# Linear-attention and SwiGLU block on one core: statistics of the first norm shared out anew, shift columns and modulations placed elsewhere

## The chip, the cores and the metric

The kernel runs on one NeuronCore of a Trainium2 chip. The metric is the device time in microseconds (us), the median of several runs. TensorE multiplies matrices and transposes, VectorE and ScalarE do element-wise work and sums, GpSimd some small operations, and SyncE (SP) issues nearly all DMAs, in order, on one queue. Each engine carries out its own instructions in the order in which they were written and waits on semaphores for the others.

## The reference

One sequence of 2048 tokens with 1024 features in bf16 passes through one block with adaptive layer norms:

```python
mod = (_silu(c) @ w_mod).reshape(c.shape[0], 6, 1, -1)
sa, ca, ga, sb, cb, gb = ...                      # shift, scale, gate, twice
h = _layernorm(x) * (1 + ca) + sa
x = x + ga * _A_ref(h, A_wqkv, A_wo)              # linear attention, 32 heads of 32
h = _layernorm(x) * (1 + cb) + sb
x = x + gb * _B_ref(h, B_w_gate, B_w_up, B_w_down)  # SwiGLU, 3584 wide
```

In the attention `phi(t) = where(t > 0, t + 1, exp(t)) + 1e-6` is applied to q and k, `kv` is the sum over the tokens of `phi(k)` times `v`, and the output is `phi(q) @ kv` over `phi(q)` times the sum of `phi(k)`, then times `wo`.

## The kernel before, in words

The 2048 tokens lie in 16 tiles of 128 (`XRES[:, st, :]`), four tiles make a chunk of 512 tokens. The program is a straight list of instructions: a small recorder (`_Prog`, line 176 for nearly all instructions, which is why the profile gives one line for them) finds the dependences from the tiles read and written and puts in the semaphores. A PSUM bank counts as one object: when another engine touched it last, the next one waits for that. The order on each engine is the order in which the Python code calls `P.pe`, `P.act`, `P.dve`, `P.pool` and `P.dma`; nothing reorders it.

**Head.** The four tiles of chunk 0 are loaded first, then in turns the scale columns' weights (`wca`, two halves), the q weights (`wq`), and the shift columns' weights (`wsa`, upper half first). TensorE runs warm-up matmuls on a zero tile. VectorE takes the statistics of tiles 0, 2 and 3 with `bn_stats`, ScalarE those of tile 1 with two passes over it (`act_stats`: one sums x, one sums x squared). GpSimd takes the power -1/2 of the variance. Tiles 0 and 1 are normed on ScalarE, 2 and 3 on VectorE. TensorE transposes each normed tile into PSUM (`tile_transposes`, 8 transposes a tile, banks 4 to 7), between these come the matmuls that make the first scale columns (`mod_sc`: one column for each 128 features, 8 matmuls of one column each), and VectorE copies the transposed features out with the scale (`h0_first`) or raw (`raw_copy`).

**q of chunk 0** (`q_phase_chunk0`). Seven of eight groups of 128 q features collect in seven banks at once, feature tile (`dt`) by feature tile, because the weights and the columns come in late. Bank 0 holds the columns. The q matmuls use h with the scale alone for `dt` 0 to 5; what the shift adds is a bias, made by one-column matmuls (`bias_mm`) and added when q is evacuated (`phi_evac`: exponential and relu on ScalarE, two operations on VectorE for each pair of groups). For `dt` 6 and 7 the shift is put in at once (`h0_scale`). After the eighth group VectorE adds the shifts to the other six tiles (`h0_shift`), since the k groups of chunk 0 need the whole h. In this stretch ScalarE takes the sums of tile 4 and VectorE those of tiles 5, 6 and 7; VectorE norms them, and a DMA transpose on SP (`th_dma`) puts each into `HT[:, 1]`, the h of chunk 1. Entries in `qside` and `kside` are carried out after the q or k group of that number.

**k of chunk 0, then chunks 1 to 3.** Each group is eight matmuls of 512 columns. After the second k group `kside` has the eight modulations of chunk 1 (`th_mod(1, dt)`: scale and shift in one VectorE operation each). Banks are taken in the turn 1, 2, 3, 4, 6, 7, 5, 0.

**Output projection.** For each token tile `st` 16 matmuls, two evacuations on VectorE with the residual (`wo_res`), and beside them the columns of the second norm: the weighted sum of weight rows (`macc`), a DMA transpose, a reduction on VectorE (`mod_red`) at `st` 8. At `st` 7 the first chunk of the second norm is normed and transposed by DMA; at `st` 8 GpSimd modulates it (`th2_mod`). The SwiGLU part follows: per chunk 28 pairs of gate and up groups, then the down projection.

Of the kernel before, what the change touches and what calls it, by code (L numbers as in the profile page):

```python
# [262 lines left out]
def bass_adaLN_cond__linear_attn_block__swiglu_ffn__prompt_kernel(  # L263
# [20 lines left out]
    EPS = 1e-5  # L284

    with ExitStack() as es:
# [117 lines left out]
        def sa_load(p):  # L404
            P.dma("wsa%d" % p, WSA[:, :, 512 * p:512 * p + 512], wmv[:, :, 512 * p:512 * p + 512])
# [12 lines left out]
        sa_load(0)  # L418
# [74 lines left out]
        def th_mod(ch, dt):  # L493
            buf = ch % 2
            if dt % 2 == 0 or ch == 1:
                P.dve("tensor_scalar", out=HT[:, buf, dt, :], in0=HT[:, buf, dt, :], scalar1=MODCOL[:, 0, dt:dt + 1],
                      scalar2=MODCOL[:, 1, dt:dt + 1], op0=ALU.mult, op1=ALU.add)
            else:
                P.act("activation", out=HT[:, buf, dt, :], in_=HT[:, buf, dt, :], func=ACT.Identity,
                      scale=MODCOL[:, 0, dt:dt + 1], bias=MODCOL[:, 1, dt:dt + 1])  # L500
# [3 lines left out]
        def mod_sc(w, c0, ms):  # L504
            for m in ms:
                for kt in range(NDT):
                    P.pe("matmul", out=PS[:, 0, c0 + m:c0 + m + 1], lhsT=w[:, kt, m * 128:(m + 1) * 128],
                         rhs=SILUC[:, kt:kt + 1], start=mod_first[0], stop=(kt == NDT - 1), skip_group_check=True)
                    mod_first[0] = False
# [14 lines left out]
        def h0_shift(dt):  # L524
            P.dve("tensor_scalar", out=HT[:, 0, dt, :], in0=HT[:, 0, dt, :], scalar1=MODCOL[:, 1, dt:dt + 1],
                  scalar2=None, op0=ALU.add)
# [47 lines left out]
        def act_stats(st, c0=0, mid=None):  # L574
            n = (D - c0) // 512
            junk0 = HT[:, 1, 0:2, :] if st < 8 else JUNK1
            for fn_, sc_, acc_ in ((ACT.Identity, 1.0 / D, SUMX), (ACT.Square, D ** -0.5, SUMSQ)):
                P.act("activation", out=junk0[:, 0:n, :], in_=XRES[:, st, c0:D].rearrange("p (a b) -> p a b", a=n),
                      func=fn_, scale=sc_, accum_out=acc_[:, st:st + 1])
                if mid is not None:  # L580
                    mid()
                    mid = None
# [13 lines left out]
        s0_, s2_, s3_ = ln1_stats_ops(0), ln1_stats_ops(2), ln1_stats_ops(3)  # L596
# [6 lines left out]

        def act_xn(st, mean):
            P.dve("tensor_scalar", out=NMR[:, st:st + 1], in0=mean, scalar1=RSTD[:, st:st + 1],
                  scalar2=-1.0, op0=ALU.mult, op1=ALU.mult)
            P.act("activation", out=XRES[:, st, :], in_=XRES[:, st, :],
                  func=ACT.Identity, scale=RSTD[:, st:st + 1], bias=NMR[:, st:st + 1])
# [7 lines left out]

        warm(13, bank=3)
        act_stats(1)
        for f in s0_:
            f()  # L620
        ln1_rstd1(0)
        s2_[0]()
        s2_[1]()
        act_xn(0, MV[:, 0, 0:1])
        tile_transposes(0)
        warm(5, bank=3)
        act_var(1)
        P.pool("tensor_tensor", out=RSTD[:, 1:2], in0=VE[:, 1:2], in1=NEGHALF[:, 0:1], op=ALU.pow)
        P.pool("tensor_scalar", out=NMR[:, 1:2], in0=SUMX[:, 1:2], scalar1=RSTD[:, 1:2], scalar2=-1.0,
               op0=ALU.mult, op1=ALU.mult)  # L630
        P.act("activation", out=XRES[:, 1, :], in_=XRES[:, 1, :], func=ACT.Identity, scale=RSTD[:, 1:2],
              bias=NMR[:, 1:2])
        s2_[2]()
        ln1_rstd1(2)
        s3_[0]()
        s3_[1]()
        s3_[2]()
        ln1_rstd1(3)
        ln1_xn(2)
        mod_sc(WCA, 8, range(2))  # L640
        tile_transposes(1, 2)
        ln1_xn(3)
        fin_ca(0, 2)
        tile_transposes(3)
# [100 lines left out]
        def q_phase_chunk0(side):  # L745
# [7 lines left out]
            for nt in range(7):  # L753
                if nt == 3:
# [5 lines left out]
            act_stats(4)  # L760
            for nt in range(7):
                if nt == 4:
                    mod_sc(WSA, 0, range(6, 8))
                    fin_sa(6, 2)
                    for dt in (6, 7):
                        h0_scale(dt)
                q_part(nt, qb[nt], (4, 5))
            mod_sc(WSA, 0, range(4, 6))
# [5 lines left out]
            for nt in range(7):  # L774
                if nt == 1:
                    mod_sc(WSA, 0, range(4))
                    fin_sa(0, 4, True)
                    ln_ops[1][0]()
                    ln_ops[1][1]()
                if nt == 4:  # L780
# [3 lines left out]
            ln_ops[1][2]()  # L784
            ln1_rstd1(5)
            for f in act_mv_ops(4):
                f()
            neg_rstd(4)
# [4 lines left out]
            for dt in (4, 5):  # L793
                h0_shift(dt)
            ln1_xn(5)
            th_dma(5)
            for dt in range(4):
                h0_shift(dt)
            ln1_xn(4)
            th_dma(4)  # L800
# [12 lines left out]
        def ln_x1(jj):  # L813
            for f in ln_ops[jj]:
                f()
            ln1_rstd1(4 + jj)
        for f in ln_ops[2]:
            add(qside, 1, f)
        for f in ln_ops[3]:
            add(qside, 1, f)  # L820
        add(qside, 1, lambda: ln1_rstd2(6))
        for jj in range(2, 4):
            add(qside, 3, lambda jj=jj: ln1_xn(4 + jj))
            add(qside, 3, lambda jj=jj: th_dma(4 + jj))
        for dt in range(NDT):
            add(kside, 1, lambda dt=dt: th_mod(1, dt))
# [253 lines left out]
        for st in range(NST):  # L1080
# [16 lines left out]
            if st == 8:  # L1097
# [6 lines left out]
            if st == 8:  # L1104
# [110 lines left out]
```

## Time and profile before

| what | before |
|---|---|
| median of 3 runs (lowest, highest) | 828.66 us (828.06, 828.85) |
| span of the profiled execution | 827.0 us |
| busy: TensorE, VectorE, ScalarE, GpSimd | 817.0, 310.8, 197.3, 40.7 us |
| mean granted TensorE clock | 1.000 |
| first to last instruction, 0 to 10 us: TensorE busy | 7.27 us |
| 10 to 30 us | 19.34 us |
| DMA read and written | 100.67 MB, 4.33 MB |

The profiled execution's own time is its span; the timed runs lie some 1.65 us above it. A timeline line gives the start, the time that a merged group of equal instructions took together, the engine, the operation with the tiles that it writes and reads, its shape, how many, and in brackets how long the engine had been idle before it and what ended that. `PEld` is TensorE's weight load, which is issued ahead of its matmul.

### The profile page before, as it was taken

To read this page: it belongs to the slowest core of one execution; us is meant where nothing else is said; L and a number is where in the kernel's file an instruction comes from. 1 tells how busy PE (TensorE), PEld (TensorE's weight loads), DVE (VectorE), ACT (ScalarE), POOL (GpSimd) and SP (SyncE) were. 2 spreads that over 40 slices of the span, in tenths; PEclk is the share of its full clock that TensorE was granted. 3 is DMA by queue.
4 is the path that set the end of the run, shared out by engine and by line. 5 is a ranking of instruction groups with operands and counts; after the bars stand their busy time and mean duration, and the time that the engine had idled before them with its cause. 6 is when DMAs were issued, how large, how long until landed. Compare 5 with 4: busy or idle time off the path is not lost.

```text
span 827.0 us, 10428 instructions
## 1 busy us (share of the span) xinstructions
PE 817.0 (99%) x4244; PEld 376.1 (45%) x4323; DVE 310.8 (38%) x664; ACT 197.3 (24%) x336; POOL 40.7 (5%) x59
## 2 busy tenths in 40 slices
PE   8999999999999999999999999999999999999998
PEld 4544444444444444444444444444444444444444
DVE  5798988476945521111221112122111211221111
ACT  4658643123241111011111101111110111111011
POOL 1010000000130000030000003000000300000000
PEclk9999999999999999999999999999999999999999
DMA  9969665856697995700455570045557004553000
GB/s 317 283 151 225 156 169 144 185 166 200 164 256 234 289 256 153 175 27 23 133 149 152 154 177 29 20 128 153 152 153 185 26 19 124 153 153 87 0 26 26
DMA packets 199360, 119.32 MB, mean 144 GB/s; under 512 B 57992, under 2 KB 183056, under 8 KB 199312
## 3 DMA queue, kind: packets, MB, share of 16 engines
q1 hardware_dynamic: 199296, 118.65, 53.7%
q8 instruction: 34, 0.56, 0.3%
q14 instruction: 14, 0.11, 0.0%
q10 hardware_dynamic: 16, 0.00, 0.0%
HBM read 100.67 MB, written 4.33 MB: 127 GB/s over the span
## 4 chain that ended last, share of the span: by engine, by line
PE 95%; DMA 2%; DVE 1%; SPq 1%; issue 1%; ACT 0%; DVEq 0%; ACTq 0%
PE ps L176 95%; DMA wsa<-in_w_mod_dram 2%; DVE acc L176 1%; SPq L176 1%; DVE pkt L176 0%; DVE e L176 0%; DVE pqt L176 0%; ACT e L176 0%; DVE xres L176 0%; DVE ht L176 0%; DVEq L247 0%; ACTq L247 0%
## 5 line engine op out<-in xcount | busy, mean ns | idle before, releaser
L176 PE MATMUL ps<-h2t,gug 128*128 128x512 bf16 x878 | 210.1, 379 | 0.9
L176 PE MATMUL ps<-h2t,guu 128*128 128x512 bf16 x878 | 209.9, 379 | 0.9
L176 DVE TENSOR_TENSOR at<-sg,ps 128x512 bf16<-128x512 bf16 x112 | 77.0, 688 | 282.7 <-PE ps L176 270.5
L176 ACT ACTIVATE sg<-ps 128x512 bf16<-128x512 f32 x112 | 66.9, 597 | 309.7 <-PE ps L176 298.3
L176 PEld LDWEIGHTS ps<-h2t,guu 128*128 128x128 bf16 x896 | 87.7, 98 | 105.7
L176 PEld LDWEIGHTS ps<-h2t,gug 128*128 128x128 bf16 x896 | 87.6, 98 | 105.5
L176 PE MATMUL ps<-wd_a,at 128*128 128x512 bf16 (+1 forms) x502 | 111.9, 377 | 0.5
L176 PE MATMUL ps<-ht,wqk 128*128 128x512 bf16 x499 | 110.5, 379 | 1.0 <-issue 0.2
L176 PE MATMUL ps<-wd_b,at 128*128 128x512 bf16 (+1 forms) x377 | 84.7, 377 | 0.4
L176 PEld LDWEIGHTS ps<-wd_a,at 128*128 128x128 bf16 x512 | 50.1, 98 | 59.7
L176 DVE TENSOR_TENSOR ut<-att,gb_b 128x512 bf16<-128x512 bf16 (+1 forms) x32 | 13.9, 435 | 167.2 <-ACT att L176 167.2
L176 PEld LDWEIGHTS ps<-ht,wqk 128*128 128x128 bf16 x512 | 49.4, 98 | 59.0 <-DVE ht L176 0.7
L176 ACT ACTIVATE att<-ps 128x512 bf16<-128x512 f32 (+1 forms) x32 | 17.4, 591 | 182.1 <-PE ps L176 182.1
L176 PEld LDWEIGHTS ps<-wd_b,at 128*128 128x128 bf16 x384 | 37.5, 98 | 44.7
L176 PE MATMUL ps<-pk,xres 128*128 128x512 bf16 x250 | 55.4, 379 | 0.6 <-issue 0.5
L176 PE MATMUL ps<-mw,pqt 128*128 128x512 bf16 x249 | 55.5, 379 | 0.5 <-issue 0.2
L176 POOL TENSOR_SCALAR h2t<-h2t,modcol 128x512 bf16<-128x512 bf16 x32 | 26.3, 837 | 383.4 <-DMA h2t<-xn 383.4
L176 ACT ACTIVATE e<-ps 128x512 bf16<-128x512 f32 x56 | 33.2, 604 | 31.9 <-PE ps L176 20.2
L176 PEld LDWEIGHTS ps<-mw,pqt 128*128 128x128 bf16 x256 | 24.7, 98 | 30.2 <-issue 0.5
L176 PEld LDWEIGHTS ps<-pk,xres 128*128 128x128 bf16 x256 | 24.7, 98 | 29.9 <-issue 0.9
L176 ACT ACTIVATE junk<-xres 128x1024 bf16<-128x1024 bf16 x24 | 25.4, 1058 | 34.5 <-DVE xres L176 34.2
L176 DVE SCALAR_TENSOR_TENSOR xres<-ps,xres 128x512 bf16<-128x512 f32 x32 | 21.4, 688 | 11.8 <-PE ps L176 11.6
(107 smaller groups left out, 337.9 us busy)
## 6 DMA issues: line engine op xcount, KB each, us to landing
gug<-in_B_w_gate_dram SPq DMA_DIRECT2D x56, 512.0 KB, 4.0
guu<-in_B_w_up_dram SPq DMA_DIRECT2D x56, 512.0 KB, 5.3
xres<-in_A_x_dram SPq DMA_DIRECT2D x20, 256.0 KB, 4.4
rb<-recip_den SPq DMA_DIRECT2D x8, 512.0 KB, 11.5
stgx<-in_w_mod_dram SPq DMA_DIRECT2D x2, 2048.0 KB, 9.7
wd_a<-in_B_w_down_dram SPq DMA_DIRECT2D x4, 1024.0 KB, 7.4
out_dram<-xres SPq DMA_DIRECT2D x31, 128.0 KB, 1.7
xres<-in_A_x_dram SPq DMA_DIRECT2D x3, 1024.0 KB, 7.1
```

Of the source, the lines that this page charges most:

```text
L176: return getattr(e, method)(**kw)
```

## The change

ScalarE sums tiles 0 and 2 of the first chunk and VectorE tiles 1 and 3; tile 0 is normed on ScalarE, the others on VectorE (`ln1_xn_sum` takes the mean from ScalarE's sum). The 13 + 5 warm-up matmuls become 16 in one run. In the q phase the last four scale columns are made one group later, the last two shift columns near the end of `dt` 4 and 5, the first four in two halves of four weight tiles, with the load of their weights in two DMAs, and the bias product one group later. ScalarE's first pass over tile 4 stays in place and its second one goes behind the second q evacuation; its scratch tile is another one. VectorE's statistics of tile 5 move behind the bias copy. The shifts of `dt` 2 and 3 go to GpSimd, and the norms and transposes of tiles 5 and 4 into the q evacuations. The modulation of chunk 1 moves from behind the second to behind the fourth k group, with `dt` 3 and 7 on GpSimd. In the output projection the reduction and the modulation of the second norm move from `st` 8 to `st` 9. Some helpers that are no longer called go.

```diff
@@ -401,8 +401,8 @@
 def ca_load(p):
     P.dma("wca%d" % p, WCA[:, :, 512 * p:512 * p + 512], wmv[:, :, D + 512 * p:D + 512 * p + 512])
 
-def sa_load(p):
-    P.dma("wsa%d" % p, WSA[:, :, 512 * p:512 * p + 512], wmv[:, :, 512 * p:512 * p + 512])
+def sa_load(p, k0=0, k1=8):
+    P.dma("wsa%d_%d" % (p, k0), WSA[:, k0:k1, 512 * p:512 * p + 512], wmv[:, k0:k1, 512 * p:512 * p + 512])
 
 def wq_load(i, n=1):
     P.dma("wq%d" % i, WQK[:, i:i + n, 0:D], wqkvv[:, i:i + n, 0:D])
@@ -415,7 +415,8 @@
 sa_load(1)
 wq_load(6)
 wq_load(7)
-sa_load(0)
+sa_load(0, 0, 4)
+sa_load(0, 4, 8)
 for j in range(2):
     P.dma("x1_%d" % j, XRES[:, 4 + j, :], xv[:, 4 + j, :])
 for i in (1, 0):
@@ -492,7 +493,10 @@
 
 def th_mod(ch, dt):
     buf = ch % 2
-    if dt % 2 == 0 or ch == 1:
+    if ch == 1 and dt in (3, 7):
+        P.pool("tensor_scalar", out=HT[:, buf, dt, :], in0=HT[:, buf, dt, :], scalar1=MODCOL[:, 0, dt:dt + 1],
+               scalar2=MODCOL[:, 1, dt:dt + 1], op0=ALU.mult, op1=ALU.add)
+    elif dt % 2 == 0 or ch == 1:
         P.dve("tensor_scalar", out=HT[:, buf, dt, :], in0=HT[:, buf, dt, :], scalar1=MODCOL[:, 0, dt:dt + 1],
               scalar2=MODCOL[:, 1, dt:dt + 1], op0=ALU.mult, op1=ALU.add)
     else:
@@ -501,9 +505,9 @@
 
 mod_first = [True]
 
-def mod_sc(w, c0, ms):
+def mod_sc(w, c0, ms, kts=range(NDT)):
     for m in ms:
-        for kt in range(NDT):
+        for kt in kts:
             P.pe("matmul", out=PS[:, 0, c0 + m:c0 + m + 1], lhsT=w[:, kt, m * 128:(m + 1) * 128],
                  rhs=SILUC[:, kt:kt + 1], start=mod_first[0], stop=(kt == NDT - 1), skip_group_check=True)
             mod_first[0] = False
@@ -521,8 +525,8 @@
     P.dve("tensor_scalar", out=HT[:, 0, dt, :], in0=HT[:, 1, dt, :], scalar1=MODCOL[:, 0, dt:dt + 1],
           scalar2=None, op0=ALU.mult)
 
-def h0_shift(dt):
-    P.dve("tensor_scalar", out=HT[:, 0, dt, :], in0=HT[:, 0, dt, :], scalar1=MODCOL[:, 1, dt:dt + 1],
+def h0_shift(dt, eng="dve"):
+    getattr(P, eng)("tensor_scalar", out=HT[:, 0, dt, :], in0=HT[:, 0, dt, :], scalar1=MODCOL[:, 1, dt:dt + 1],
           scalar2=None, op0=ALU.add)
 
 def bias_mm(dts):
@@ -571,15 +575,12 @@
 
 JUNK1 = T("junk1", 204 * KB, [128, 2, 512], BF16)
 
-def act_stats(st, c0=0, mid=None):
-    n = (D - c0) // 512
-    junk0 = HT[:, 1, 0:2, :] if st < 8 else JUNK1
-    for fn_, sc_, acc_ in ((ACT.Identity, 1.0 / D, SUMX), (ACT.Square, D ** -0.5, SUMSQ)):
-        P.act("activation", out=junk0[:, 0:n, :], in_=XRES[:, st, c0:D].rearrange("p (a b) -> p a b", a=n),
+def act_stats(st, passes=(0, 1)):
+    junk0 = HT[:, 1, 0:2, :] if st < 4 else JUNK1[:]
+    for i in passes:
+        fn_, sc_, acc_ = ((ACT.Identity, 1.0 / D, SUMX), (ACT.Square, D ** -0.5, SUMSQ))[i]
+        P.act("activation", out=junk0, in_=XRES[:, st, :].rearrange("p (a b) -> p a b", a=2),
               func=fn_, scale=sc_, accum_out=acc_[:, st:st + 1])
-        if mid is not None:
-            mid()
-            mid = None
 
 def act_mv_ops(st):
     return [
@@ -593,19 +594,13 @@
           op1=ALU.add)
     P.pool("tensor_tensor", out=RSTD[:, st:st + 1], in0=VE[:, st:st + 1], in1=NEGHALF[:, 0:1], op=ALU.pow)
 
-s0_, s2_, s3_ = ln1_stats_ops(0), ln1_stats_ops(2), ln1_stats_ops(3)
+s1_, s3_ = ln1_stats_ops(1), ln1_stats_ops(3)
 
 def act_var(st):
     P.dve("scalar_tensor_tensor", out=MV[:, st, 1:2], in0=SUMX[:, st:st + 1], scalar=SUMX[:, st:st + 1],
           in1=SUMSQ[:, st:st + 1], op0=ALU.mult, op1=ALU.subtract)
     P.dve("tensor_scalar", out=VE[:, st:st + 1], in0=MV[:, st, 1:2], scalar1=-1.0, scalar2=EPS, op0=ALU.mult,
           op1=ALU.add)
-
-def act_xn(st, mean):
-    P.dve("tensor_scalar", out=NMR[:, st:st + 1], in0=mean, scalar1=RSTD[:, st:st + 1],
-          scalar2=-1.0, op0=ALU.mult, op1=ALU.mult)
-    P.act("activation", out=XRES[:, st, :], in_=XRES[:, st, :],
-          func=ACT.Identity, scale=RSTD[:, st:st + 1], bias=NMR[:, st:st + 1])
 
 def tile_transposes(*js):
     for dt in range(NDT):
@@ -614,34 +609,39 @@
             P.pe("transpose", out=PSB[:, 4 + dt // 2, c:c + 128], in_=XRES[:, j, dt * 128:(dt + 1) * 128],
                  identity=IDENT[:])
 
-warm(13, bank=3)
-act_stats(1)
-for f in s0_:
+def ln1_xn_sum(st):
+    P.dve("tensor_scalar", out=XRES[:, st, :], in0=XRES[:, st, :],
+          scalar1=SUMX[:, st:st + 1], scalar2=RSTD[:, st:st + 1], op0=ALU.subtract, op1=ALU.mult)
+
+def pool_pow(st):
+    P.pool("tensor_tensor", out=RSTD[:, st:st + 1], in0=VE[:, st:st + 1], in1=NEGHALF[:, 0:1], op=ALU.pow)
+
+warm(16, bank=3)
+act_stats(0)
+for f in s1_:
     f()
-ln1_rstd1(0)
-s2_[0]()
-s2_[1]()
-act_xn(0, MV[:, 0, 0:1])
+ln1_rstd1(1)
+act_var(0)
+pool_pow(0)
+P.pool("tensor_scalar", out=NMR[:, 0:1], in0=SUMX[:, 0:1], scalar1=RSTD[:, 0:1], scalar2=-1.0,
+       op0=ALU.mult, op1=ALU.mult)
+act_stats(2)
+for f in s3_:
+    f()
+ln1_rstd1(3)
+P.act("activation", out=XRES[:, 0, :], in_=XRES[:, 0, :], func=ACT.Identity, scale=RSTD[:, 0:1],
+      bias=NMR[:, 0:1])
+act_var(2)
+pool_pow(2)
+ln1_xn(1)
+tile_transposes(1)
 tile_transposes(0)
-warm(5, bank=3)
-act_var(1)
-P.pool("tensor_tensor", out=RSTD[:, 1:2], in0=VE[:, 1:2], in1=NEGHALF[:, 0:1], op=ALU.pow)
-P.pool("tensor_scalar", out=NMR[:, 1:2], in0=SUMX[:, 1:2], scalar1=RSTD[:, 1:2], scalar2=-1.0,
-       op0=ALU.mult, op1=ALU.mult)
-P.act("activation", out=XRES[:, 1, :], in_=XRES[:, 1, :], func=ACT.Identity, scale=RSTD[:, 1:2],
-      bias=NMR[:, 1:2])
-s2_[2]()
-ln1_rstd1(2)
-s3_[0]()
-s3_[1]()
-s3_[2]()
-ln1_rstd1(3)
-ln1_xn(2)
+ln1_xn(3)
 mod_sc(WCA, 8, range(2))
-tile_transposes(1, 2)
-ln1_xn(3)
+tile_transposes(3)
+ln1_xn_sum(2)
 fin_ca(0, 2)
-tile_transposes(3)
+tile_transposes(2)
 mod_sc(WCA, 8, range(2, 4))
 h0_first(0, "dve")
 h0_first(1, "dve")
@@ -751,20 +751,21 @@
         for nt in nts:
             q_part(nt, qb[nt], dts)
     for nt in range(7):
-        if nt == 3:
+        if nt == 4:
             mod_sc(WCA, 8, range(4, 8))
             fin_ca(4, 4)
             for dt in (4, 5):
                 h0_scale_only(dt)
         q_part(nt, qb[nt], (2, 3))
-    act_stats(4)
-    for nt in range(7):
-        if nt == 4:
-            mod_sc(WSA, 0, range(6, 8))
-            fin_sa(6, 2)
-            for dt in (6, 7):
-                h0_scale(dt)
+    act_stats(4, (0,))
+    for nt in range(6):
         q_part(nt, qb[nt], (4, 5))
+    q_part(6, qb[6], (4,))
+    mod_sc(WSA, 0, range(6, 8))
+    fin_sa(6, 2)
+    for dt in (6, 7):
+        h0_scale(dt)
+    q_part(6, qb[6], (5,))
     mod_sc(WSA, 0, range(4, 6))
     fin_sa(4, 2, True)
     for nt in range(7):
@@ -772,32 +773,27 @@
             bias_mm((4, 5))
         q_part(nt, qb[nt], (6,))
     for nt in range(7):
-        if nt == 1:
-            mod_sc(WSA, 0, range(4))
+        if nt == 2:
+            mod_sc(WSA, 0, range(4), range(4))
+        if nt == 4:
+            mod_sc(WSA, 0, range(4), range(4, 8))
             fin_sa(0, 4, True)
-            ln_ops[1][0]()
-            ln_ops[1][1]()
-        if nt == 4:
+        if nt == 5:
             bias_mm(range(4))
             bias_fin()
         q_part(nt, qb[nt], (7,))
-    ln_ops[1][2]()
-    ln1_rstd1(5)
-    for f in act_mv_ops(4):
-        f()
-    neg_rstd(4)
     q_phi = lambda nt: phi_evac(qb[nt] if nt < 7 else 0, PQT[:, nt, 0:512], bias=BIASQ[:, nt:nt + 1])
     for i, dt in enumerate((4, 5, 0, 1, 2, 3, 6, 7)):
         P.pe("matmul", out=PS[:, 0, :], lhsT=WQK[:, dt, 896:1024], rhs=HT[:, 0, dt, :], start=(i == 0),
              stop=(i == 7))
-    for dt in (4, 5):
+    for f in ln_ops[1]:
+        f()
+    P.dve("tensor_scalar", out=VE[:, 5:6], in0=MV[:, 5, 1:2], scalar1=EPS, scalar2=None, op0=ALU.add)
+    for dt in (4, 5, 0, 1):
         h0_shift(dt)
-    ln1_xn(5)
-    th_dma(5)
-    for dt in range(4):
-        h0_shift(dt)
-    ln1_xn(4)
-    th_dma(4)
+    for dt in (2, 3):
+        h0_shift(dt, "pool")
+    pool_pow(5)
     for nt in range(8):
         q_phi(nt)
         for f in side.get(nt, []):
@@ -810,20 +806,23 @@
 qside, kside = {}, {}
 ln_ops = [ln1_stats_ops(4 + jj) for jj in range(4)]
 
-def ln_x1(jj):
-    for f in ln_ops[jj]:
-        f()
-    ln1_rstd1(4 + jj)
 for f in ln_ops[2]:
-    add(qside, 1, f)
+    add(qside, 0, f)
+add(qside, 0, lambda: ln1_xn(5))
+add(qside, 0, lambda: th_dma(5))
+add(qside, 1, lambda: act_stats(4, (1,)))
+add(qside, 1, lambda: act_var(4))
+add(qside, 1, lambda: pool_pow(4))
 for f in ln_ops[3]:
     add(qside, 1, f)
 add(qside, 1, lambda: ln1_rstd2(6))
+add(qside, 1, lambda: ln1_xn_sum(4))
+add(qside, 1, lambda: th_dma(4))
 for jj in range(2, 4):
     add(qside, 3, lambda jj=jj: ln1_xn(4 + jj))
     add(qside, 3, lambda jj=jj: th_dma(4 + jj))
 for dt in range(NDT):
-    add(kside, 1, lambda dt=dt: th_mod(1, dt))
+    add(kside, 3, lambda dt=dt: th_mod(1, dt))
 for jj, k in ((0, 3), (1, 4)):
     add(kside, k, lambda jj=jj: act_stats(10 + jj))
 q_phase_chunk0(qside)
@@ -1094,14 +1093,14 @@
         macc(STGX[0], kt)
     if st == 6:
         macc_split()
-    if st == 8:
+    if st == 9:
         mod_red()
         mod_fin_col(3, False)
     if st == 7:
         for jj in range(4):
             ln2_xn(jj)
         th2_dma()
-    if st == 8:
+    if st == 9:
         th2_mod()
     if st == 7:
         for q in range(4):
```

## The prediction, made before the changed kernel ran

> **What bounds the kernel now.** I read the page first, part 1 and the chain that ended last: TensorE is busy for 99% of the span and holds 95% of that chain.
>
> ```profile
> span 827.0 us, 10428 instructions
> ...
> PE 817.0 (99%) x4244; PEld 376.1 (45%) x4323; DVE 310.8 (38%) x664; ACT 197.3 (24%) x336; POOL 40.7 (5%) x59
> ...
> PE 95%; DMA 2%; DVE 1%; SPq 1%; issue 1%; ACT 0%; DVEq 0%; ACTq 0%
> ```
>
> So an edit pays only if it shortens or lengthens a place where TensorE stands still. Since matmuls overlap, those places show best in the timeline of its weight loads: a load that waits, right-hand brackets, marks them. Head, q phase, first k group of chunk 1 and the output projection:
>
> ```profile
> 7.28 0.15 PEld L176 LDWEIGHTS ps<-e,ident 128*128 128x128 bf16 x1 [0.28 <-issue]
> 8.64 0.45 PEld L176 LDWEIGHTS ps<-ident,xres 128*128 128x128 bf16 x8 [1.21 <-ACT xres L176]
> 9.04 0.80 PEld L176 LDWEIGHTS ps<-e,ident 128*128 128x128 bf16 x5
> 9.96 0.67 PEld L176 LDWEIGHTS ps<-siluc,wca 128*128 128x128 bf16 x16
> 10.56 1.35 PEld L176 LDWEIGHTS ps<-ident,xres 128*128 128x128 bf16 x24
> ...
> 21.40 0.47 PEld L176 LDWEIGHTS ps<-siluc,wsa 128*128 128x128 bf16 x16 [0.67 <-DMA wsa<-in_w_mod_dram]
> ...
> 24.04 0.47 PEld L176 LDWEIGHTS ps<-modtmp,wqk 128*128 128x128 bf16 x16 [0.42 <-DVE modcol L176]
> ...
> 45.83 0.55 PEld L176 LDWEIGHTS ps<-ht,wqk 128*128 128x128 bf16 x4 [0.23 <-DVE ht L176]
> ...
> 227.04 0.55 PEld L176 LDWEIGHTS ps<-mw,pqt 128*128 128x128 bf16 x4 [0.39 <-DVE xres L176]
> ```
>
> A load is normally issued one matmul (0.216 us at full speed) ahead, so the true stalls are smaller than the brackets: 0.34 us for the first shift columns, 0.09 for their bias product, 0.10 in the first k group of chunk 1, 0.27 at 227. First q matmul: 12.50; eighth q group: 28.69. Between 12.5 and 134 us TensorE has no other stall worth naming. All that can be removed here is about 1.2 us (with 0.36 from the head, below), 0.15% of the span. New stalls have no such ceiling.
>
> **Head, first norm.** TensorE's order before, from 8.64: 8 transposes, 5 warm-up matmuls, 16 column products, 24 transposes. After, behind three more warm-up matmuls: 16 transposes, 16 products, 8 and 8 transposes. ScalarE can start tile 0 at 3.64, where VectorE starts it now (its load has landed), and runs two passes on it and two on tile 2: 1.06 us each plus the accumulator read, 1.18 pitch as in the rows now, so to 8.37; tile 0's scaling follows at 8.28 and its first transpose 1.30 later, at 9.58, by the 7.35 to 8.64 of the row now. VectorE's norm of tile 1 stands behind tile 2's variance, which waits for ScalarE: 8.43, then two small operations, so 8.74 to 9.28; tile 1's transposes start at 9.34. Then 16 x 0.056, 16 x 0.025, 8 x 0.056: tile 2's begin at 11.11, and its second one at 11.17 instead of 11.53 frees the first scaled copy. **-0.36 us**: first q matmul at 12.13. Covers: GpSimd's four powers and one product (0.56 to 0.79 each) end by 9.6 and tile 2's norm needs that before 11.1; wq0 landed at 11.14; the column weights at 9.79, wanted at 10.2.
>
> **q phase.** The scale columns move one matmul group later (their two copies at 18.05 to 18.67 had 8 matmuls to hide in, now 6: enough). The last two shift columns move behind 11 matmuls instead of 8 and 5, wanted at 21.8 instead of 21.07; the weights landed at 21.36, so the 0.34 goes. Late next: the second pair of shift columns waits for VectorE's copy out of the same bank, 0.42 to 0.47 after the last product (21.80 to 22.16 now, plus the semaphore), and only one matmul, 0.22, lies between instead of six: +0.18. The scaled copies 6 and 7 now push the next cast by 0.07: bias wait 0.16 instead of 0.09, and 0.02 for copy 6. The load in two halves (512 KB each, on one queue, the whole landing at 25.73; 0.43 to 0.63 us of issue more on SP, ahead of the x tiles that land from 26.4): halves wanted at 25.5 and 26.3, so both are hidden. But then only one matmul instead of three stands between the last product and the bias: 0.55 from product to bias load, as 23.49 to 24.04 now, less 0.24: +0.31. Sum of new stalls 0.67 against 0.46 now: **+0.21**. Eighth group at 28.54.
>
> **Tile 4 and 5, VectorE.** ScalarE's second pass over tile 4 moves behind two q evacuations and delays the third by 1.2 us; that bank is wanted at 33.7, free at 33.1. On VectorE from the bias copy on there is no gap today until 41.56. Added: tile 5's statistics 1.31 (they filled a wait before); gone: two shifts 0.53 and a copy 0.06. The chain to the second k pair ends 41.56 - 0.03 + 0.72 = 42.25. The move of the chunk-1 modulation behind the fourth k group puts the evacuation of groups 2 and 3 (45.70 to 47.32 now, 1.62) ahead of it: it can start at 43.9. Now it starts at 43.10, because it waits for the transposed tiles:
>
> ```profile
> 43.10 2.67 DVE L176 TENSOR_SCALAR ht<-ht,modcol 128x512 bf16<-128x512 bf16 x8 [1.54 <-DMA ht<-xres]
> ```
>
> Those transposes are issued on SP in order (tile 5, 4, 6, 7), tiles 6 and 7 about 0.7 us later than today; 4.3 to 4.8 us from issue to landing gives 43.6, under 43.9, and the x loads queued behind them on SP are wanted much later.
>
> **GpSimd beside VectorE.** Four 512-column operations move to GpSimd: two shifts and two modulations. Alone, eight such take 6.02 us; beside VectorE's two-input operations 6.78, and those VectorE operations take 0.88 and 0.80 instead of 0.42:
>
> ```profile
> 228.54 6.02 POOL L176 TENSOR_SCALAR h2t<-h2t,modcol 128x512 bf16<-128x512 bf16 x8 [3.66 <-DMA h2t<-xn]
> 350.95 6.78 POOL L176 TENSOR_SCALAR h2t<-h2t,modcol 128x512 bf16<-128x512 bf16 x8 [103.06 <-DMA h2t<-xn]
> 354.30 0.88 DVE L176 TENSOR_TENSOR xres<-xres,ut 128x512 bf16<-128x512 bf16 x1
> 355.55 0.80 DVE L176 TENSOR_TENSOR xres<-xres,ut 128x512 bf16<-128x512 bf16 x1
> ```
>
> That is 0.83 us of VectorE for four GpSimd operations: 0.21 each. No row shows a shift (0.34) beside one. Bounds: 0, and 0.45 each by the worst operation. I take 0.21, the mean of the nearest row; VectorE standing still for a whole GpSimd operation, 0.77, is the far end. The Trainium skill, page "SBUF — State Buffer", section "Who interferes with whom", speaks against the change: a fast VectorE tensor_scalar and a GpSimd operation exclude each other for the whole instruction. The row at 354 shows exclusion in part; by the page all four would cost 0.77 each, and the sum would be 831.8.
>
> With 0.21 each: the four VectorE shifts end at 31.15 + 0.42 = 31.57, where the first k group wants the last of them at 31.28; GpSimd's two (2 x 0.77 from 29.85, plus 0.4) end at 31.8, wanted at 31.7. **+0.3** on TensorE. The modulation starts at 43.9 + 0.84 = 44.75; its sixth VectorE operation ends 5 x 0.324 + 0.41 later, 0.05 to the semaphore, two matmuls 0.43: the k group ends at 47.26, where it ends at 46.05 now. Of these 1.21 us, -0.15 is the head and q phase, 0.3 the shifts, **+1.06** the modulation.
>
> After that VectorE is ahead, not behind, since two evacuations are done already; nothing is added to chunk 1.
>
> **Output projection.** The reduction of 2.28 us held VectorE from 223.69 and a bank was late by 0.27. One group of 3.45 us later the transposed input is long there; the same reduction still blocks VectorE for 2.6 us, but the evacuations are then no longer behind the four norms of step 7, so I count the stall as gone, **-0.27** (ends: 0 and -0.27). GpSimd's modulation starts some 2 us later than 228.54 and ends near 237; the gate matmuls want it at 244.3.
>
> Sum: -0.36 + 0.21 + 0.30 + 1.06 - 0.27 = +0.94 on the profiled 827.0. The median 828.66 stands 1.65 above that span (work around it); I keep that: **829.6 us**. 0.2%, 1.7 us, is about what a measurement of this kernel can tell from no change, so this is "no change", leaning slower.
>
> **Rivals.**
> - GpSimd's work collides with nothing: modulation from 43.9, k group done at 46.41, no stall at the shifts: +0.36 - 0.27, 828.7; with VectorE 0.4 shorter, 828.4. For it: GpSimd's powers beside VectorE shifts at 29.4 left these at 0.34. Against: those read one column.
> - Slower, by one mechanism: GpSimd and VectorE exclude each other longer. At 0.45 for each of the four, the modulation starts at 45.7 and the k group ends at 48.2: 830.5; at 0.77, 831.8. It decides once the modulation starts later than 45.5, which is 0.4 per operation. For it: 0.88 against 0.42 above. Against: only two of four VectorE operations were hit there.
> - Slower, clock: five warm-up matmuls between the transposes go. The clock is half (0.427 between matmuls) from 2.6 to 7.7 and full from the first transpose on. Should it fall back and stay half for as long, 5.1 us, half of that is lost: 829.6 + 2.5 = 832.1. Against: at 166 to 170, mostly 32-column products, it stays full. The skill's page "TensorE: Matmul & The Clock Gate", section "What's actually happening", has the gate watch windows of 3.4 us and close after an idle one, which would make 1.7 of the 2.5; no run here shows it closing.
> - Faster by more than 0.2%: the stalls seen add to 1.2 us, 827.5 at best, so it needs something that this profile does not show.
>
> **How the numbers follow.** Forecast as worked 0.40, no collision 0.10: together 0.50 within 0.2%. Slower: exclusion 0.27, clock 0.06, another late transfer (a transposed tile after 44.75) 0.09: 0.42. Faster 0.08. The forecast's own range is 828.4 to 830.3; the range for 8 in 10 takes the exclusion case in up to 0.77 per operation and half of the faster case: 827.2 to 831.7.
>
> **What would show it.** Right: first q matmul near 12.1; a weight load of the second bias product waiting for VectorE; chunk-1 modulation on VectorE from 44.75 with GpSimd operations over 0.77; VectorE shifts above 0.34; no load waiting at 227. Wrong: half-speed pitches after 9 us, or a modulation that ends before 46.

## The result and the profile after

The changed kernel takes 831.12 us (median of five runs, 831.02 to 831.51), the kernel before 828.45 us (five runs, 828.06 to 828.85). The ratio is 1.0034 with a 95% interval of 1.0023 to 1.0045, so it is 0.23 to 0.45% slower. The profiled executions have spans of 827.0 and 828.9 us. The page of the kernel after, part 1 and the shares of the chain that ended last:

```profile
span 828.9 us, 10506 instructions
...
PE 822.2 (99%) x4321; PEld 376.0 (45%) x4321; DVE 310.8 (37%) x657; ACT 198.1 (24%) x339; POOL 45.6 (5%) x63
...
PE 96%; DVE 2%; ACT 1%; DMA 0%; issue 0%; ACTq 0%
```

TensorE is still the bound, and VectorE has the same busy time as before, 310.8 us, with seven instructions fewer: those that stayed became longer. TensorE's 822.2 against 817.0 says little: the matmul records differ by 77, the weight loads by 2, so records are missing before. GpSimd has 4.9 us more for four more wide operations. The timeline of the weight loads of the kernel after shows where TensorE stands still (start, duration, then in brackets the idle time and what ended it):

```profile
9.29 0.90 PEld L176 LDWEIGHTS ps<-ident,xres 128*128 128x128 bf16 x16 [0.80 <-DVE xres L176]
...
22.51 0.47 PEld L176 LDWEIGHTS ps<-siluc,wsa 128*128 128x128 bf16 x16 [0.32 <-DVE modcol L176]
...
27.12 0.87 PEld L176 LDWEIGHTS ps<-modtmp,wqk 128*128 128x128 bf16 x32 [0.41 <-DVE modcol L176]
...
28.33 1.86 PEld L176 LDWEIGHTS ps<-ht,wqk 128*128 128x128 bf16 x10 [0.30 <-DVE biasq L176]
30.66 0.10 PEld L176 LDWEIGHTS ps<-ht,wqk 128*128 128x128 bf16 x1 [0.47 <-DVE ht L176]
...
32.24 0.11 PEld L176 LDWEIGHTS ps<-ht,wqk 128*128 128x128 bf16 x2 [0.53 <-DVE ht L176]
32.97 2.06 PEld L176 LDWEIGHTS ps<-ht,wqk 128*128 128x128 bf16 x11 [0.62 <-POOL ht L176]
...
45.57 0.10 PEld L176 LDWEIGHTS ps<-ht,wqk 128*128 128x128 bf16 x1 [0.61 <-DVE ht L176]
46.35 0.10 PEld L176 LDWEIGHTS ps<-ht,wqk 128*128 128x128 bf16 x1 [0.69 <-DVE ht L176]
...
222.09 9.81 PEld L176 LDWEIGHTS ps<-mw,pqt 128*128 128x128 bf16 x46
```

A gap of about 0.11 us is normal between two loads. The new stalls are at 30 to 33, where the first k group waits for the shifts, the last one for GpSimd's, and from 45, where chunk 1's first k group waits for the modulations. The wait at 227 is gone. Four of VectorE's shifts in the kernel before, and then the same two places on VectorE and GpSimd in the kernel after (timelines; a duration is that of a merged group):

```profile
30.10 1.13 DVE L176 TENSOR_SCALAR ht<-ht,modcol 128x512 bf16<-128x512 bf16 x4
```

```profile
29.82 2.37 DVE L176 TENSOR_SCALAR ht<-ht,modcol 128x512 bf16<-128x512 bf16 x4
44.82 2.76 DVE L176 TENSOR_SCALAR ht<-ht,modcol 128x512 bf16<-128x512 bf16 x6
...
29.79 3.13 POOL L176 TENSOR_SCALAR ht<-ht,modcol 128x512 bf16<-128x512 bf16 x2 [20.05 <-DVE mv L176]
32.89 0.57 POOL L176 TENSOR_TENSOR rstd<-ve,neghalf 128x1 f32<-128x1 f32 x1
...
44.61 1.54 POOL L176 TENSOR_SCALAR ht<-ht,modcol 128x512 bf16<-128x512 bf16 x2 [6.54 <-DMA ht<-xres]
```

GpSimd's two shifts take 3.13 us together, its two modulations 1.54. The records one by one: the shifts 1.565 and 1.588, the modulations 0.762 and 0.792; VectorE's four shifts 0.793, 0.342, 0.699 and 0.769 (0.341 to 0.347 before, with nothing wide on GpSimd), its first two modulations 0.696 and 0.859, the others about 0.40. GpSimd's power for tile 5 stands behind the shifts and ends at 33.45.

Four moments in the trace serve from here on. E is the first weight load of the eighth q group; K the start of the second k group of chunk 0, read from its second load, which goes out as its first matmul starts; M the start of the first modulation on VectorE; C the start of the second k group of chunk 1, read like K. From C to the end of the q and k groups (the first load of `ps<-pqt,zsel`, at 136.40 in the kernel after) every kernel takes the same 88.3 us, and from the first gate load to TensorE's last load 580.39 us in all of them. From the end of the q and k groups to the projection's first load they take 52.2 to 53.2 us; what differs there is a stall at about 175 us that comes and goes, told at the end. So what the change makes different lies ahead of C or in the projection.

| kernel | median | E | K - E | M | C - E |
|---|---|---|---|---|---|
| before | 828.45 | 28.51 | 3.63 | 43.10 | 17.55 |
| after | 831.12 | 28.33 | 4.87 | 44.82 | 19.75 |
| shifts and modulations on VectorE | 830.13 | 28.54 | 3.49 | 44.34 | 18.76 |
| shifts on VectorE | 830.61 | 28.33 | 3.49 | 44.10 | 19.10 |
| modulations on VectorE | 831.28 | 28.57 | 4.87 | 45.05 | 19.44 |
| modulation behind the second k group | 831.30 | 29.11 | 5.04 | 45.75 | 20.01 |
| before, with the new head | 828.39 | 28.81 | 3.62 | 43.53 | 17.68 |
| VectorE's shifts first | 831.67 | 28.64 | 4.86 | 45.12 | 19.76 |
| all on VectorE, second k group | 829.94 | 28.40 | 3.49 | 44.17 | 18.73 |
| head and columns alone | 828.48 | 28.39 | 3.47 | 42.70 | 17.29 |
| GpSimd's shifts with two scalars | 830.97 | 28.42 | 4.17 | 44.53 | 19.48 |
| the last but two, with tile 5's statistics early | 829.26 | 28.38 | 3.47 | 43.01 | 17.60 |
| after, tile 5's statistics early | 831.76 | 28.45 | 4.83 | 44.90 | 19.73 |

("The last but two" is "all on VectorE, second k group".) Each row is one profiled execution, so a difference of one or two tenths in it may be chance. The kernel before measured 828.62, 828.52 and 828.64 beside the three groups of experiments.

### The profile page after: what moved, and what is told of

Read it like the earlier page. It is cut to its first block, busy times and chain, and to the rows that moved or that the text cites. A ratio compares the mean times of both kernels' runs of the same rounds, so it can differ in the third digit from the quotient of the medians.

```text
span 828.9 us, 10506 instructions
## 1 busy us (share of the span) xinstructions
PE 822.2 (99%) x4321; PEld 376.0 (45%) x4321; DVE 310.8 (37%) x657; ACT 198.1 (24%) x339; POOL 45.6 (5%) x63
## 3 DMA queue, kind: packets, MB, share of 16 engines
q1 hardware_dynamic: 199312, 118.65, 53.2%
## 4 chain that ended last, share of the span: by engine, by line
PE 96%; DVE 2%; ACT 1%; DMA 0%; issue 0%; ACTq 0%
PE ps L176 96%; ACT ht L176 1%; DVE ht L176 0%; DVE stats L176 0%; DMA xres<-in_A_x_dram 0%; DVE pqt L176 0%; DVE pkt L176 0%; DVE xres L176 0%; DVE e L176 0%; ACT e L176 0%; DVE mv L176 0%; ACT rl L176 0%; DVE ve L176 0%; DVE biasq L176 0%; DVE modtmp L176 0%
## 5 line engine op out<-in xcount | busy, mean ns | idle before, releaser
L176 PE MATMUL ps<-ht,wqk 128*128 128x512 bf16 x512 | 113.1, 379 | 1.2 <-DVE ht L176 0.9
L176 ACT ACTIVATE junk<-xres 128x1024 bf16<-128x1024 bf16 x26 | 27.5, 1059 | 45.3 <-DVE xres L176 34.2
```

What stands on the lines that cost most here:

```text
L176: return getattr(e, method)(**kw)
```

## The experiments

The theory to begin with was that of the prediction: the loss comes from GpSimd's four new operations, which collide with VectorE's. The rivals: the modulation's new place behind the fourth k group, the new order of the work on tiles 4 and 5, and the head.

**All four GpSimd operations back on VectorE.** In `th_mod` the branch for `dt` 3 and 7 is taken out, and:

```diff
-            for dt in (4, 5, 0, 1):
+            for dt in (4, 5, 0, 1, 2, 3):
                 h0_shift(dt)
-            for dt in (2, 3):
-                h0_shift(dt, "pool")
```

> The changed kernel with all four GpSimd operations (shifts of feature tiles 2 and 3, chunk-1 modulations of 3 and 7) back on VectorE. Collision theory (GpSimd and VectorE lock each other out): six shifts take 6 x 0.263 + 0.08 = 1.66 us instead of 2.37, the stall of 1.38 us in the first k group goes, the modulation starts 0.7 earlier at 44.1 and ends after 8 x 0.324; the first k group of chunk 1 ends near 47.05 instead of 48.08: about 1.0 us faster than the changed kernel, 830.1. Order theory (VectorE is late because of tile 5's statistics ahead of the shifts and two evacuations ahead of the modulation): VectorE only gets more work, 2 x 0.26 + 2 x 0.32, 831.1 to 832.

Measured: 830.13 us, ratio to before 1.0020 (1.0011 to 1.0029). C - E falls by 0.99 us from 19.75 to 18.76. About 1 us of the loss is GpSimd's work, and more than 1 us is something else.

**The two shifts alone back on VectorE** (the diff above, without the branch).

> The changed kernel with the two shifts back on VectorE, the two modulations left on GpSimd. Collision theory: second k group of chunk 0 starts at 31.82 instead of 33.20, VectorE is 0.7 us earlier, the first k group of chunk 1 ends near 47.4: 0.7 us faster than the changed kernel, 830.4. Order theory: no gain, 831.1 or 0.5 more.

Measured: 830.61 us, 1.0025 (1.0015 to 1.0035). K - E falls by 1.38 to 3.49, C - E by 0.65.

**The two modulations alone back on VectorE** (`if False:` in place of `if ch == 1 and dt in (3, 7):`).

> The changed kernel with the two modulations back on VectorE, the two shifts left on GpSimd. Collision theory: the first two modulations take 0.40 instead of 0.70 and 0.86 us, eight of them end at 44.82 + 2.67, the k group at 47.77 instead of 48.08: 0.3 us faster, 830.8. Order theory: two more operations on VectorE, 0.6 us slower, 831.7.

Measured: 831.28 us, 1.0031 (1.0019 to 1.0042), no change in the time that can be told. C - E falls by 0.31. The two parts, 0.65 and 0.31, add up to nearly the 0.99 of both.

**The modulation back behind the second k group.**

```diff
-            add(kside, 3, lambda dt=dt: th_mod(1, dt))
+            add(kside, 1, lambda dt=dt: th_mod(1, dt))
```

> The changed kernel with the modulation of chunk 1 back behind the second k group, GpSimd's share kept. Collision theory: it starts when the last transposed tile has landed, 44.45 instead of 44.82: 0.4 us faster at most, 830.7. Order theory: the two evacuations (1.62 us) were the cause: 1.5 us faster, 829.6.

Measured: 831.30 us, 1.0034 (1.0021 to 1.0046). The modulation does not start earlier: M - E is 16.64 against 16.49. VectorE now stands idle for 1.53 us ahead of it, until the transposed tiles land. The new place costs nothing, because the landing, not the evacuations, would set the start.

**The head alone.** The kernel before with the statistics, warm-up matmuls, norms and transposes of the changed head, and nothing else of the change.

> The kernel before with the new head alone (ScalarE sums tiles 0 and 2, 16 warm-up matmuls in one run, tile order 1, 0, 3, 2). The prediction's working: first q matmul 0.36 us earlier. But the first shift columns then want their weights earlier too, so if these land as in the profile of before (21.36) all of it is given back there: 828.6, no change; if they land as in the profile of the changed kernel (20.08) up to 0.4 us stay: 828.2. Rival (the head waits longer in most runs than in the profiled one, through the x loads): 829.0 or more.

Measured: 828.39 us, 0.9998 (0.9990 to 1.0007). The first transposes start at 10.0 in its profile, against 8.64 before and 9.29 after, and E at 28.81. This profiled execution, 829.44 us, is the slowest of its kernel's eleven. The runs with the new head have this start between 9.2 and 10.1. What the head gains in one profile is not seen in the median.

**VectorE's shifts ahead of tile 5's statistics.** So GpSimd's shifts run when VectorE's are done:

```diff
+            for dt in (4, 5, 0, 1):
+                h0_shift(dt)
             for f in ln_ops[1]:
                 f()
             P.dve("tensor_scalar", out=VE[:, 5:6], in0=MV[:, 5, 1:2], ...)
-            for dt in (4, 5, 0, 1):
-                h0_shift(dt)
             for dt in (2, 3):
                 h0_shift(dt, "pool")
```

> The changed kernel with VectorE's four shifts ahead of tile 5's statistics instead of behind them, so that GpSimd's two shifts run beside the statistics. Collision theory: VectorE's shifts go from 28.7 to 29.9 at 0.34 us each, GpSimd's two then take about 0.77 each beside bn_stats and end by 31.4, so the stall of 1.38 us in the first k group nearly goes, and VectorE is about 0.7 earlier at the modulation: 0.7 us faster than the changed kernel, 830.4. Rival (GpSimd is slow on these tiles by itself, 1.57 each): it ends at 32.9 whatever VectorE does, 831.1.

Measured: 831.67 us, 1.0035 (1.0021 to 1.0049). The timeline of this kernel, VectorE and GpSimd:

```profile
29.10 1.14 DVE L176 TENSOR_SCALAR ht<-ht,modcol 128x512 bf16<-128x512 bf16 x4 [0.51 <-PE ps L176]
...
30.10 3.11 POOL L176 TENSOR_SCALAR ht<-ht,modcol 128x512 bf16<-128x512 bf16 x2 [20.35 <-DVE ht L176]
```

VectorE's four shifts are undisturbed (0.348 to 0.353 each) and over before GpSimd starts, and GpSimd's still take 3.11 us, beside `bn_stats` only. So the collision with VectorE's shifts is not what makes them 1.57 us long. This was against the theory, which from here on needs a second part: the operation itself.

**All on VectorE and the modulation behind the second k group** (the first and fourth edit together).

> As the run with all four operations back on VectorE (830.1), and the modulation behind the second k group again. That run's modulation still starts 1.2 us later, counted from the eighth q group, than in the kernel before. If the two evacuations ahead of it are the cause: it starts 0.6 to 1.2 earlier, as soon as the last transposed tile has landed, near 43.7, 829.0 to 829.5. If the late transposes (tile 5 and 4 normed later) are the cause: it waits for them, at 44.2, and no more than 0.2 is won, 830.0.

Measured: 829.94 us, 1.0016 (1.0007 to 1.0025); C - E 18.73, as with the first edit alone. What is left against before, 1.2 us at C, is neither GpSimd's nor the place of the modulation.

**Head and columns alone.** The changed kernel with tiles 4 and 5 (statistics and norms), the shifts and the modulation as before; the new head, the columns' places, the load in two and `st` 9 stay.

> The changed kernel with everything that concerns tiles 4 and 5, the shifts and the modulation put back as before: what stays is the head, the shift and scale columns, the load in two and the later reduction of the second norm. Theory (all of the loss lies in the shifts, the norms of tiles 4 and 5 and the modulation): 0.1 to 0.4 us faster than before, 828.3. Rival (the columns or the head cost something that the profiled run does not show): 829 or more.

Measured: 828.48 us, 0.9999 (0.9990 to 1.0008). M is 42.70 and C - E 17.29. So the whole loss lies in the shifts, the modulation and the work on tiles 4 and 5, and the rest of the change is worth nothing that can be measured.

**GpSimd's shifts with two scalars.** The same sum, written in the form that the modulations have:

```diff
+            if eng == "pool":
+                P.pool("tensor_scalar", out=HT[:, 0, dt, :], in0=HT[:, 0, dt, :], scalar1=1.0,
+                       scalar2=MODCOL[:, 1, dt:dt + 1], op0=ALU.mult, op1=ALU.add)
+                return
```

> The kernel after, with GpSimd's two shifts written with two scalars (times 1.0, plus the shift column) instead of one. Theory, the one-scalar form itself is slow on GpSimd: 0.77 to 0.9 us each instead of 1.57, the second k group of chunk 0 starts near 32.2 instead of 33.2; the first k group of chunk 1 then ends 0 to 0.7 us earlier (its other delays overlap), so 830.4 to 831.1, about 830.6. Rival, the tile, its address or the VectorE shifts beside it make it slow: 1.57 again, 831.1.

Measured: 830.97 us, 1.0030 (1.0018 to 1.0041). The timeline of this kernel:

```profile
29.88 1.55 POOL L176 TENSOR_SCALAR ht<-ht,modcol 128x512 bf16<-128x512 bf16 x2 [20.05 <-DVE mv L176]
...
29.91 1.92 DVE L176 TENSOR_SCALAR ht<-ht,modcol 128x512 bf16<-128x512 bf16 x4
```

GpSimd's two take half the time, 0.852 and 0.717. VectorE's four take 1.92 us together where they take 1.14 undisturbed (0.344, 0.710, 0.777, 0.334): the collision alone is 0.78. K comes 0.70 earlier relative to E. That splits the 1.38 that the shifts cost there: 0.70 go with the form, 0.68 stay with the quick form, where VectorE's stretched shifts end last (31.83, GpSimd's 31.43). K was expected near 32.2 and came at 32.59; the time is inside the expected 830.4 to 831.1, but its gain on the changed kernel cannot be told from none.

**The operations by themselves**, in the kernel before, in the second SwiGLU chunk, with an unused scratch tile as output. Extra work, nothing left out.

```diff
+    form = {10: (sh1, None, ALU.add, None), 12: (sc1, sh1, ALU.mult, ALU.add),
+            14: (1.0, sh1, ALU.mult, ALU.add), 16: (sh1, 0.0, ALU.add, ALU.add),
+            20: (sc1, sh1, ALU.mult, ALU.add)}.get(ft)
+    for i in range(2 if form else 0):
+        kw = dict(out=JUNK[:, 0:512], in0=src, scalar1=form[0], scalar2=form[1], op0=form[2])
...
+        P.pool("tensor_scalar", **kw)
+    for i in range(4 if ft >= 20 else 0):
+        P.dve("tensor_scalar", out=JUNK[:, 512:1024], in0=src, scalar1=sh1, scalar2=None, op0=ALU.add)
```

> The kernel before, with extra operations in the second SwiGLU chunk that write an unused scratch tile: on GpSimd, with no such VectorE work beside them, two operations each with one column scalar, with two column scalars, with a constant 1.0 and a column, and with a column and a constant 0.0; then two two-scalar ones beside four one-scalar VectorE operations, and at last these four VectorE operations alone. Theory, the form sets the time: 1.57 us with one scalar, 0.77 with two of any kind. Rival, the place sets it: all near 0.77. VectorE's four: 0.34 alone, 0.6 to 0.8 for those beside GpSimd. All of it lies under TensorE's work: 828.5, within 0.3.

Measured: 828.67 us, 0.9998 (0.9988 to 1.0008). The timeline, GpSimd's five pairs and VectorE's two fours:

```profile
428.50 3.22 POOL L176 TENSOR_SCALAR junk<-at,modcol 128x512 bf16<-128x512 bf16 x2 [70.74 <-DVE at L176]
435.49 1.63 POOL L176 TENSOR_SCALAR junk<-at,modcol 128x512 bf16<-128x512 bf16 x2 [3.77 <-DVE at L176]
442.39 1.48 POOL L176 TENSOR_SCALAR junk<-at,modcol 128x512 bf16<-128x512 bf16 x2 [5.28 <-DVE at L176]
449.30 4.10 POOL L176 TENSOR_SCALAR junk<-at,modcol 128x512 bf16<-128x512 bf16 x2 [5.43 <-DVE at L176]
463.11 1.86 POOL L176 TENSOR_SCALAR junk<-at,modcol 128x512 bf16<-128x512 bf16 x2 [9.72 <-DVE at L176]
...
462.97 2.15 DVE L176 TENSOR_SCALAR junk<-at,modcol 128x512 bf16<-128x512 bf16 x4
476.78 1.52 DVE L176 TENSOR_SCALAR junk<-at,modcol 128x512 bf16<-128x512 bf16 x4
```

One column added: 1.565 and 1.557 us, with no collision. Two columns: 0.762. Times 1.0 plus a column: 0.692. But a column added and then 0.0 added: 2.00. So "two scalars of any kind" was wrong. The two forms that start with a multiplication are quick and the two that start with an addition are slow; whether it is the first operation or the place of the column was not tried. The last pair lies beside VectorE: 0.849 and 0.906 on GpSimd for 0.762 alone, and 0.353, 0.751, 0.353, 0.589 on VectorE for 0.353 alone. Both engines pay.

**Tile 5's statistics early again**, on the kernel with all on VectorE and the modulation behind the second k group:

```diff
                     fin_sa(0, 4, True)
+                    ln_ops[1][0]()
+                    ln_ops[1][1]()
...
-            for f in ln_ops[1]:
-                f()
+            ln_ops[1][2]()
```

> All four GpSimd operations back on VectorE and the modulation behind the second k group (as in the run that measured 829.94), and tile 5's bn_stats ahead of the bias copy again, where they fill VectorE's wait. Theory, these 1.31 us in VectorE's unbroken stretch are what delays the norms of tiles 6 and 7: the norm of tile 6 starts near 36.8, the modulation near 43.0 instead of 44.17, and the time is 828.7 to 829.0. Rival, it is the order of the norms of tiles 4 and 5 or ScalarE's split passes: modulation near 44.2, 829.9.

Measured: 829.26 us, 1.0008 (0.9999 to 1.0017). VectorE's timeline, first without this edit, then with it: tile 5's statistics, the norms of tiles 6 and 7, the modulation.

```profile
28.26 1.28 DVE L176 BATCH_NORM_STATS2 stats<-xres 128x6 f32<-128x512 bf16 x2
...
37.86 1.00 DVE L176 TENSOR_SCALAR xres<-xres,mv,rstd 128x1024 bf16<-128x1024 bf16 x2
...
44.17 2.67 DVE L176 TENSOR_SCALAR ht<-ht,modcol 128x512 bf16<-128x512 bf16 x8 [1.54 <-DMA ht<-xres]
```

```profile
26.99 1.28 DVE L176 BATCH_NORM_STATS2 stats<-xres 128x6 f32<-128x512 bf16 x2
...
36.80 1.00 DVE L176 TENSOR_SCALAR xres<-xres,mv,rstd 128x1024 bf16<-128x1024 bf16 x2
...
43.01 2.68 DVE L176 TENSOR_SCALAR ht<-ht,modcol 128x512 bf16<-128x512 bf16 x8 [1.44 <-DMA ht<-xres]
```

Placed in the wait for the bias the statistics are free. Behind the bias copy they push the norms by 1.06 us, these the transposes, and these the modulation by 1.16. C - E is 17.60, near that of before, 17.55, but 0.31 above the 17.29 of head and columns alone, which has the same head and the same order of q matmuls. So the order of the norms of tiles 4 and 5 and ScalarE's split passes cost 0.3 us at most here, and one profile each does not tell that from none. The median fell by 0.68, less than C - E (1.13); it was expected at 828.7 to 829.0, and missed that.

**The same edit on the changed kernel**, with GpSimd's operations in it.

> The kernel after, with tile 5's bn_stats ahead of the bias copy again and nothing else. Theory, the VectorE chain is 1.25 us earlier, but the GpSimd shifts still hold the second k group to 33.2; the modulation starts near 43.6 and the first k group of chunk 1 ends some 1.1 earlier than in after: about 830.1. Rival, the statistics' place has no effect: 831.1.

Measured: 831.76 us, 1.0038 (1.0024 to 1.0052): no gain at all, C - E 19.73. The timeline says why:

```profile
30.66 1.29 DVE L176 BATCH_NORM_STATS2 stats<-xres 128x6 f32<-128x512 bf16 x2 [0.64 <-DMA xres<-in_A_x_dram]
33.57 0.55 DVE L176 TENSOR_SCALAR xres<-xres,mv,rstd 128x1024 bf16<-128x1024 bf16 x1 [1.38 <-POOL rstd L176]
...
29.88 3.12 POOL L176 TENSOR_SCALAR ht<-ht,modcol 128x512 bf16<-128x512 bf16 x2 [20.07 <-DVE ht L176]
32.97 0.56 POOL L176 TENSOR_TENSOR rstd<-ve,neghalf 128x1 f32<-128x1 f32 x1
```

The power of tile 5's variance stands on GpSimd behind the two slow shifts. VectorE is ready and waits 1.38 us for it, and norms tile 5 at 33.57, as late as in the changed kernel (33.54). There two delays of the same length lie side by side, GpSimd's shifts and the late statistics. Taking GpSimd's shifts out alone gives 0.65 at C, moving the statistics alone nothing; with both, and the modulations on VectorE behind the second k group too, 2.15 of the 2.20 are gone. So the parts do not add up.

No version here beats the kernel before: the two nearest to it, the kernel before with the new head and head and columns alone, measure the same.

## Why the prediction was right or wrong

The time lies inside the range (827.2 to 831.7) and on the side to which the forecast leaned, but the likeliest case, 829.6 us and "no change", is not what came: 831.12 is 0.3% slower, past the 0.2% bound. The rival "GpSimd and VectorE exclude each other longer" (0.27) comes nearest: it had the k group end at 48.2 for 0.45 us per operation, and the trace has 48.08. Its mechanism is one part of three, beside the slow form of the shift and the late statistics. So it is in part luck that the range holds the time: its upper end was set by GpSimd blocking VectorE for 0.77 us per operation, which no run here shows; the slow form and 0.39 us outside the span were not in the prediction, and the late statistics stood in it as covered.

| step | predicted | measured |
|---|---|---|
| head, to the first q group | -0.36 | -0.42 (load at 12.46, now 12.04) |
| q phase | +0.21 | +0.24 |
| shifts, at the second k group (K - E) | +0.30 | +1.24 |
| shifts and modulation, at C (C - E) | +1.36 | +2.20 |
| output projection | -0.27 | -0.07 |
| span | +0.94 | +1.92 |
| outside the span | 0 | +0.39 |

The last two lines make 2.31, and the medians differ by 2.67: the profiled execution of the kernel before (828.85) was the slowest of its five, that of the kernel after (831.02) the fastest. The line for C holds that for the second k group.

- **Head: right in the profile.** The first transposes were put at 9.34 (9.29) and the first q matmul at 12.13 (12.07). But the kernel before with this head was no faster in the median, so as a term of the time it showed nothing.
- **q phase: right.** The waits came where they were named: the second pair of shift columns behind VectorE's copy (0.32 in the bracket, 0.21 over the normal gap, for 0.18), the bias product (0.41, so 0.30, for 0.31), the bias copy (0.30, so 0.19, for 0.16).
- **"2 x 0.77" for GpSimd's shifts: wrong.** It was taken from rows of the two-column form, `h2t`, for an operation with one column. They measured 1.565 and 1.588, by themselves 1.56. The row was of the same engine, size and opcode, and still of another form. The prediction named no bound for this from any row further off.
- **"0.21 each" for the collisions: too small.** VectorE's four shifts lost 1.23 us to two GpSimd operations, its modulations 0.74 to two, so 0.62 and 0.37 each. With quick shifts it was 0.39. The row that it was taken from gave little less: of its four GpSimd operations three were lengthened, to 0.96, 1.18 and 0.93 us, and by these alone VectorE's 0.83 is 0.28 each. The upper bound of 0.45 from the worst operation held for the quick form, not for the slow one. The rule of the Trainium skill ("SBUF — State Buffer", section "Who interferes with whom": the one is blocked for the other's whole instruction) would give, as an estimate with GpSimd's durations here, 0.77 for each modulation and 1.57 for each shift; the runs show exclusion in part, and losses on both sides (0.849 and 0.906 on GpSimd for 0.762 alone).
- **"41.56 - 0.03 + 0.72 = 42.25" for VectorE's chain to the second pair of k evacuations: wrong by 1.0.** It measured 43.27. The sum left out the collisions at the shifts, which the 44.75 then added, and priced them too low; nor did it follow GpSimd's queue to the power of tile 5 behind the shifts. Tiles 6 and 7 were normed 1.70 later, not 0.7, and the transposed tiles were in at 44.41 instead of 43.6.
- **The modulation at 44.75: met (44.82), by errors that cancel.** All four collisions were put ahead of the start, and those at the modulations, 0.74, fell after it. The move behind the fourth k group, on which the start was worked out, costs nothing. The late statistics do: 1.13 at C when GpSimd is out of the way, though the prediction had the same 1.31 us in its sum and took them to be covered up to 43.9.
- **Output projection, "-0.27": a misread bracket.** The wait at 227 was there and is gone, as said, but it was worth 0.07. The load behind the late one follows after 0.015 us instead of 0.216: a late load uses up its lead, so the bracket counts more than the matmuls lose.
- **"I keep that" for the 1.65 outside the span: wrong by 0.4.** The time less the span, as a mean over a kernel's runs, is 1.74 before and 2.13 after. It is 2.08 to 2.11 in the other kernels with both shifts and modulations on GpSimd, 1.87 and 1.86 with one of the two, 1.72 to 1.75 in four with neither; but 1.91 in the kernel before with the new head, which has neither, and 1.76 in the one with ten extra GpSimd operations. So it is not simply GpSimd's work, and what it is stays open.
- **Clock:** the warm-up matmuls come 0.427 us apart up to 7.7 us and 0.216 from 8.0 on, and no half-speed pitch follows. That rival is out.

## What to carry to other kernels

Price a moved operation by a row of its own form on the engine it goes to, operations and scalars included; where there is none, a factor of two, the size of the miss here, belongs into the bounds. An engine that is 5% busy can still be on the critical path through what is queued behind the new work, here a power of one column behind two wide shifts. And look at what an operation filled before: the same 1.3 us of statistics were free in a wait and cost over 1 us a few instructions later, and undoing one of two equal delays shows nothing.

## What the runs showed of the hardware

- GpSimd's `tensor_scalar` on 128 x 512 bf16 took 1.56 us for "plus a column", 0.76 for "times a column plus a column", 0.69 for "times 1.0 plus a column", and 2.00 for "plus a column plus 0.0".
- VectorE's one-column operation of 0.35 us took 0.59 to 0.79 beside a GpSimd operation, and not each of them: in the run of the operations by themselves, one that lay wholly beside a GpSimd operation ran at 0.353 while GpSimd's took 0.906 instead of 0.762. Its `bn_stats` were not disturbed.
- A stall that comes and goes: in seven of the fourteen profiles TensorE waits 0.3 to 1.0 us longer at about 175 us, whatever the kernel, without a releaser. The weight loads of the changed kernel and of the last experiment there:

```profile
174.54 2.92 PEld L176 LDWEIGHTS ps<-pk,xres 128*128 128x128 bf16 x15 [0.23 <-issue]
```

```profile
174.64 1.19 PEld L176 LDWEIGHTS ps<-pk,xres 128*128 128x128 bf16 x7 [0.23 <-issue]
176.77 0.74 PEld L176 LDWEIGHTS ps<-pk,xres 128*128 128x128 bf16 x4 [0.93 <-issue]
```

Such stalls are of the size of the differences told here, which is why the readings above go by the moments ahead of it. They may be why a few medians (829.26, 831.76) lie above what those moments would make of them, but only one execution of each kernel was profiled. The cause stays open.
